# Attention and a routed layer of eight experts on one core: narrower buffer waits, a late search of four bits a step, splits and fillers placed anew

## The chip, the core and the metric

The kernel runs on one core of a Trainium2 chip. A time is that of one execution on the device in microseconds (us). Before the change three runs gave 829.34, 824.45 and 827.95 us, a median of 827.95. One more execution was taken with the profiler.

## What is computed

The reference first computes causal attention with a position bias for 8 batches of 8 heads, 576 positions and 64 columns. The result is viewed as 4608 tokens of 512 columns, and a routed layer follows:

```python
logits = x @ w_gate                      # 4608 tokens, 8 experts
order = np.argsort(-logits.flatten())    # best pair of token and expert first
for idx in order:                        # each expert takes at most 576 tokens
    tok, e = idx // E, idx % E
    if assigned[tok] >= 0 or counts[e] >= cap: continue
    assigned[tok] = e; counts[e] += 1
for e in range(E):
    mask = assigned == e
    out[mask] = np.maximum(x[mask] @ w1[e], 0) @ w2[e]   # 512 -> 1024 -> 512
```

The assignment is sequential in the reference. The kernel finds it one expert at a time: which expert fills first, and at which logit.

## The kernel before, in words

**Order of the work.** The program is written out by a planner (`Plan`). Each instruction or small group is a task with an engine, a duration, dependencies, buffers from a `Ring`, a priority (the lower number goes first) and sometimes a slack or a hold. The planner simulates the engines. When an engine comes free it starts the task that can start soonest; the priority decides only between tasks that can start at the same moment, and after that the order in which they were entered. A task with a hold stands back if one of lower number will be ready within that time. The order so found is the order of each engine's queue on the chip, where instructions wait in turn.

**Attention** (`Attention`) runs to about 350 us. At its end `xout` stores the last batch's rows in HBM (`xs`, L616 and L618), `turn` forms the router's logits, and `batch_tasks` takes each token's best expert and the sort key's first digit (`choose`, L788 to L809). The router's constants are made by GpSimd early in attention (`consts`, L730), one after the other (`build`, L669).

**Routing** (`Router.phase`, L836) is done eight times, once per expert j, with one plan for routing and experts together. It searches the key at which an expert reaches its 576 tokens, seven steps of at most five bits (`BITS`). A step, on VectorE and TensorE in turn: compare the 40 token columns with 32 candidate digits (`ge`, L886, 1280 elements); ten matmuls count per candidate and expert (L909); copy the counts (`ca`, L913); four matmuls with `qb` add up four parts (L918); compare with the places left (`pe`, L921); one matmul counts candidates (L923); take the largest (`jc`, L926); subtract (`wd`, L930). Beside this chain `digits` cuts the next digits (L813) and L897 prepares `y`. Then the expert's number `ei` is known (L861). A prefix matmul (L982, L983) and `places` (L1018) turn marks into token numbers: VectorE steps, ten matmuls (L1051), a copy, four matmuls (L1058), and `ids` (L1065). A bookkeeping chain (L996 to L1014) and the next phase's `choose` run beside it. For j of 2 and more, search matmuls get a slack of 0.45 us (`SLACK`), so the planner sets them that much after their operands.

**Experts** (`Moe.expert`, L1090). SyncE reads `ei` and loads twelve pieces of that expert's weights (L1134). ScalarE makes the high halves (L1138), VectorE the low halves (L1141); both have priority 2 + j. GpSimd gathers the tokens by `ids` in five tiles, four of 128 and one of 64 (L1103). For expert 0 TensorE transposes each tile (L1118) and ScalarE copies it; for the others a transposing DMA on SyncE does (L1110). The first layer (`first`, L1159) has eight units of 12 matmuls of 512 columns (L1169), each followed by one of 64 for the fifth tile (L1173). With `split`, only for expert 0, three of the units are begun tile by tile as tiles arrive, in matmuls of 128 columns. Then `relu`, and the second layer (L1240, L1243), whose results GpSimd scatters (L1223).

**Filler.** `route_and_experts` (L1267) enters sixteen matmuls that compute nothing (L1280) after the first placement.

**Memory.** Attention's pools are closed before the router's and experts' pools (`Router.pools`, L724; `Moe.__init__`, L1078) are opened over the same bytes. A pool opened in the plain way makes its first users wait until all tiles of the pools that it lies over are done with.

Of the kernel before, what the change touches and what calls it, by code (L numbers as in the profile page):

```python
# [9 lines left out]
F32 = mybir.dt.float32  # L10
F16 = mybir.dt.float16
# [193 lines left out]
class Attention:  # L205
# [454 lines left out]
    def build(self):  # L660
# [8 lines left out]
        for dur, f in self.router.consts():  # L669
            x = pl.add("p", dur, f, [x], prio=3)  # L670
# [26 lines left out]
J = 32  # L697
BITS = (5, 5, 5, 5, 5, 5, 2)
# [3 lines left out]
SLACK = (0.0, 0.15, 0.45)  # L702
NONE = 1.0e9
NT = 8 * S


class Router:
# [3 lines left out]
    def __init__(self, tc, ctx, L):  # L711
        self.tc, self.nc, self.L = tc, tc.nc, L
        c = self.c = ctx.enter_context(tc.tile_pool(name="rc", bufs=1))
# [7 lines left out]
        self.dg = c.tile([128, len(BITS), NC_], I32, name="dg")  # L721
        self.w0 = c.tile([128, NC_], BF, name="w0")

    def pools(self, ctx):  # L724
        P = lambda name, bufs, **k: ctx.enter_context(self.tc.tile_pool(name=name, bufs=bufs, **k))
        self.w = P("rw", 1)
        self.out = P("ro", 1)
        self.ps = P("rps", 1, space=PSUM)

    def consts(self):  # L730
# [6 lines left out]
        def do(dur, f):  # L737
            todo.append((dur, f))
# [6 lines left out]
        self.kj = iota([128, J, 4], [[1, J], [0, 4]], base=1, dt=BF, name="kj")  # L745
        self.Ws = iota([128, len(BITS), E], [[16, len(BITS)], [-1, E]], base=16 + E, name="Ws")
# [7 lines left out]
        self.quart = T([128, 128], F16, "quart")  # L754
        fill(self.quart, 16.0)
# [5 lines left out]
        for cc in range(4):  # L761
            do(0.35, lambda cc=cc: g.affine_select(
                self.qb[:, cc].rearrange("p (a b) -> p a b", a=4), on.rearrange("p (a b) -> p a b", a=4),
                pattern=[[0, 4], [-4, J]], base=-cc, channel_multiplier=1, compare_op=OP.is_equal, fill=0.0))
# [4 lines left out]
        do(0.35, lambda: g.tensor_copy(self.ident16, self.identf))  # L769
        fill(self.U, 1.0)  # L770
# [17 lines left out]
    def choose(self, c=slice(0, NC_)):  # L788
# [5 lines left out]
        B = [128, c.stop - c.start, E]  # L794
# [12 lines left out]
            (0.175, lambda: v.tensor_scalar(dg[:, 0], sg, 32 - BITS[0], None, op0=OP.logical_shift_right)),  # L807
# [3 lines left out]
    def digits(self, c):  # L811

        return [lambda s=s, n=n: self.nc.vector.tensor_scalar(  # L813
            self.dg[:, s, c], self.sg[:, c], 32 - sum(BITS[:s + 1]), 2 ** n - 1,
            op0=OP.logical_shift_right, op1=OP.bitwise_and) for s, n in enumerate(BITS) if s]

    def rings(self):
# [3 lines left out]
            ge=R(w, [128, NC_ // 4, J, 4], F16, "ge", 2), y=R(w, [128, NC_], F32, "y", 2),  # L821
            ca=R(w, [128, 4, E], F16, "ca", 2), pe=R(w, [128, E], F16, "pe", 2), wd=R(w, [128, NC_], BF, "wd", 2),
# [513 lines left out]
```

## Time and profile before

| what | value |
|---|---|
| median of three runs | 827.95 us |
| the profiled execution | 835.8 us, its span 834.1 us |
| busy share of the span | TensorE 89%, VectorE 73%, ScalarE 46%, GpSimd 42% |
| mean granted TensorE clock | 0.942 |

A stretch is read with its granted clock: TensorE has two levels, 1.2 and 2.4 GHz, shown as 0.5 and 1. A busy share is an average over a stretch, and what limits a stretch is seen from which wait ends last in it. In a row of the order of time the first number is the start in microseconds from the span's beginning, the second the duration of one instruction or of a merged run (x tells how many); brackets tell for how long the engine stood idle before it and what it waited for. `DVE` is VectorE, `PE` TensorE, `ACT` ScalarE, `POOL` GpSimd, `SP` SyncE.

### The profile page before, as it was taken

The page shows a single profiled execution, that of the slowest core. Times are in us where ns is not written, and L with a number is a line of the kernel's source. Part 1 is how long each engine was busy: PE and PEld are TensorE (multiplying, and loading weights), DVE is VectorE, ACT ScalarE, POOL GpSimd, SP SyncE. Part 2 cuts the span into 40 slices and gives each one's busy share as a digit, 9 for nine tenths or more (in the row PEclk, how much of TensorE's full clock was granted, in tenths as well). Part 3 has the DMA queues.
Part 4 walks back from the last instruction along what each step waited for, and adds up shares of the span by engine and source line. Part 5 has one row for each costly group of instructions (what it writes and reads, how often), then busy time and mean ns, then how long its engine had stood idle before and what let it go on. Part 6 is the DMA issues. An engine that isn't in the chain of part 4 may idle for free.

```text
span 834.1 us, 23171 instructions
## 1 busy us (share of the span) xinstructions
PE 740.5 (89%) x9059; PEld 466.9 (56%) x9059; DVE 605.6 (73%) x1992; ACT 379.8 (46%) x724; POOL 348.1 (42%) x423
## 2 busy tenths in 40 slices
PE   5288999999989999624999999999999799999995
PEld 1167777877778778512854545545555355454542
DVE  7679999999999997457885786867869568550110
ACT  2366877887768766503441233422334223441210
POOL 5178878878878888302013031121322112401011
PEclk8599999999999999855799999999999999999998
DMA  4955758685657511105238266392735937961001
GB/s 138 288 146 161 229 154 229 191 227 152 195 163 214 145 32 60 58 1 181 80 128 213 72 174 162 127 226 91 187 118 149 193 93 180 262 186 39 20 14 45
DMA packets 85316, 119.30 MB, mean 143 GB/s; under 512 B 40726, under 2 KB 57238, under 8 KB 85206
## 3 DMA queue, kind: packets, MB, share of 16 engines
q1 hardware_dynamic: 79318, 98.93, 43.3%
q0 software_dynamic: 5888, 18.88, 7.9%
q8 instruction: 71, 1.16, 0.6%
q14 instruction: 39, 0.32, 0.1%
HBM read 71.67 MB, written 19.10 MB: 109 GB/s over the span
## 4 chain that ended last, share of the span: by engine, by line
PE 44%; issue 18%; DVE 17%; DMA 5%; POOL 4%; ACT 1%; another core or an unknown queue 0%; SPq 0%; POOLq 0%; DVEq 0%; ACTq 0%
PE psm L1169 13%; PE psm L1243 10%; DVE scr L442 6%; DVE QK L381 3%; PE pst L514 2%; DMA xg<-xs,ids 2%; PE pst L515 2%; PE pss L473 2%; PE psm L1240 2%; PE psn L1173 2%; PE psa L909 2%; PE po L587 2%; POOL out_dram L1223 2%; PE po L589 2%; PE po L588 1%
## 5 line engine op out<-in xcount | busy, mean ns | idle before, releaser
L527 POOL TENSOR_TENSOR R<-P 128x512 f16<-128x512 f32 (+1 forms) x224 | 236.9, 1083 | 45.0 <-ACT P L525 43.9
L1169 PE MATMUL psm<-xT,w1p 128*128 128x512 f16 (+1 forms) x876 | 197.4, 358 | 0.0
L1243 PE MATMUL psm<-w2p,hT 128*128 128x512 f16 x768 | 178.5, 383 | 0.0
L1173 PE MATMUL psn<-xT,w1p 128*128 128x64 f16 x768 | 142.2, 193 | 0.0
L525 ACT ACTIVATE P<-pst 128x512 f32<-128x512 f32 (+1 forms) x224 | 117.6, 548 | 51.4 <-PE pst L517 26.7
L442 DVE CUSTOM_DVE_ANT_0 scr<-pss,mS 128x512 bf16<-128x512 f32 (+3 forms) x256 | 124.1, 485 | 12.2 <-PE pss L473 1.8
L1169 PEld LDWEIGHTS <-w1p 128*128 128x128 f16 x876 | 81.8, 100 | 80.1
L1103 POOL DMA_INDIRECT xg<-xs,ids x40 | 42.2, 1055 | 199.1 <-DVE sg L805 96.3
L1223 POOL DMA_INDIRECT out_dram<-y,ids x40 | 41.6, 1040 | 196.1 <-ACT y L1254 164.4
L1243 PEld LDWEIGHTS <-hT 128*128 128x128 f16 x768 | 70.3, 98 | 81.1 <-issue 5.4
L587 PE MATMUL po<-V,P 128*128 128x65 f16 x960 | 110.1, 195 | 2.3 <-DVE xp L608 1.8
L514 PE MATMUL pst<-QK 70*128 70x64 f16 (+4 forms) x512 | 105.4, 249 | 7.1 <-DMA QK<-mt 6.7
L589 PE MATMUL po<-V,R 128*128 128x65 f16 x960 | 110.2, 193 | 0.1
L588 PE MATMUL po<-Vl,P 128*128 128x64 f16 x960 | 109.9, 192 | 0.0
L515 PE MATMUL pst<-QK 128*128 128x64 f16 (+4 forms) x512 | 104.9, 248 | 0.0
L587 PEld LDWEIGHTS <-P 128*128 128x128 bf16 x960 | 89.6, 97 | 9.3 <-issue 6.7
L588 PEld LDWEIGHTS <-P 128*128 128x128 bf16 x960 | 89.1, 99 | 7.3 <-issue 3.5
L1189 ACT ACTIVATE hT<-psm 128x512 f16<-128x512 f32 x64 | 38.2, 597 | 119.1 <-PE psm L1169 94.8
L473 PE MATMUL pss<-QK 67*128 67x512 f16 (+3 forms) x256 | 72.9, 307 | 20.3 <-DVE mr L442 13.5
L589 PEld LDWEIGHTS <-R 128*128 128x128 f16 x960 | 89.1, 97 | 0.3 <-POOL R L527 0.3
L1173 PEld LDWEIGHTS <-w1p 128*128 128x128 f16 x768 | 72.8, 98 | 0.7
L1254 ACT ACTIVATE y<-psm 128x512 f32<-128x512 f32 x32 | 19.1, 596 | 114.5 <-PE psm L1243 103.6
(202 smaller groups left out, 1396.0 us busy)
## 6 DMA issues: line engine op xcount, KB each, us to landing
QK<-QK SPq DMA_DIRECT2D x120, 144.0 KB
wst<-in_w_dram SPq DMA_DIRECT2D x32, 512.0 KB
wst<-in_w_dram SPq DMA_DIRECT2D x64, 256.0 KB
rv<-in_v_dram SPq DMA_DIRECT2D x16, 576.0 KB
raw<-in_q_dram SPq DMA_DIRECT2D x15, 576.0 KB
raw<-in_k_dram SPq DMA_DIRECT2D x15, 576.0 KB
xs<-xp SPq DMA_DIRECT2D x8, 1024.0 KB
xs<-xp SPq DMA_DIRECT2D x8, 128.0 KB
```

Of the source, the lines that this page charges most:

```text
L442: return pl.add("v", dur, lambda: nc.vector.tensor_tensor_reduce(scr.t[:, :n], ps(), mask, 1.0, init() if init else -3e38, OP.add, OP.max, ...
L473: nc.tensor.matmul(ps.t[:, :n], F()[:, q0:q0 + 128], F()[:, k0:k0 + n], start=True, stop=True)
L514: nc.tensor.matmul(ps[:, c0:c0 + n], F()[:, ks:ks + 128], F()[:, q:q + n], start=True, stop=False)
L515: nc.tensor.matmul(ps[:, c0:c0 + n], G()[:, ks:ks + 128], G()[:, q:q + n], start=False, stop=not diag)
L525: e = pl.add("a", n / 1200 + 0.171, lambda: nc.scalar.activation(P.t[:, c0:c0 + n], ps.t[:, :n], AF.Exp, scale=1.0 / YS), [x] + fresh, pri ...
L527: sub = lambda eng: eng.tensor_tensor(R.t[:, c0:c0 + n], P.t[:, c0:c0 + n], strided_hi(P.t)[:, c0:c0 + n], op=OP.subtract)
L587: nc.tensor.matmul(o[:, i], H[:, c:c + 128], V.t[:, pr, sl], start=f, stop=False)
L588: nc.tensor.matmul(o[:, i, 0:64], H[:, c:c + 128], Vl.t[:, pr, sl], start=False, stop=False)
L589: nc.tensor.matmul(o[:, i], R.t[:, c:c + 128], V.t[:, pr, sl], start=False, stop=l)
L1169: nc.tensor.matmul(ps[:, tiles[0]:tiles[-1] + 1] if len(tiles) > 1 else ps[:, tiles[0]], lhs(f, c, a), xT.t[:, tiles[0]:tiles[-1] + 1, 4 * ...
L1173: nc.tensor.matmul(pt.t[:, 64 * f:64 * f + 64], lhs(f, c, a), xT.t[:, 4, 4 * b + c, 0:64], start=s, stop=e)
L1243: nc.tensor.matmul(py.t, hT.t[:, f, a, 128 * i:128 * i + 128], w2p.t[:, f, b], start=f == 0 and k == 0, stop=f == 7 and k == 2)
```

## The change

- Both pools over attention's memory are opened so that each tile waits only for those earlier tiles whose bytes it covers (`reuse_waits="tile"`).
- Search has two forms. Experts 0 and 1 keep 32 candidates, four columns at a time, seven steps. Experts 2 to 6 get 16 candidates, eight columns at a time, eight steps of four bits: `ge` of 640 elements, five count matmuls of 64 columns, a product with a constant mask (`own`) in place of the copy, one matmul with a constant (`same`) in place of four, a reduction (`sm`), then as before.
- The slack of search matmuls from the third phase on goes from 0.45 to 0.3 us.
- `places` of the first phase gets priority -1 instead of 0. The splits of expert 0's W1 get 0.5 instead of 2.
- `split` holds for experts 0 and 1.
- Filler: five matmuls after the first phase's last search matmul, fourteen after its prefix, twenty-eight after its placement, instead of sixteen after the placement.
- Three new constants are made on VectorE during attention, two more on GpSimd.

The diff, cut to its core:

```diff
-BITS = (5, 5, 5, 5, 5, 5, 2)
+FEW, MANY = (32, 4, (5, 5, 5, 5, 5, 5, 2)), (16, 8, (4,) * 8)
-SLACK = (0.0, 0.15, 0.45)
+SLACK = (0.0, 0.15, 0.3)
+PW_ = (0.5,)
...
     def pools(self, ctx):
-        P = lambda name, bufs, **k: ctx.enter_context(self.tc.tile_pool(name=name, bufs=bufs, **k))
+        P = lambda name, bufs, **k: ctx.enter_context(self.tc.tile_pool(name=name, bufs=bufs, reuse_waits="tile", **k))
...
+        J, G = self.forms[1].J, self.forms[1].G
+        self.own, self.same1, self.same = T([128, G], F32, "own"), T([128, J], F32, "same1"), T([128, 128], F16, "same")
+        v, one = nc.vector, self.identf.rearrange("p (j c) -> p j c", c=G)
+        do(0.29, lambda: v.tensor_reduce(self.own, one.rearrange("p j c -> p c j"), AX.X, OP.add), "v")
+        do(0.29, lambda: v.tensor_reduce(self.same1, one, AX.X, OP.add), "v")
+        do(0.29, lambda: v.tensor_copy(self.same.rearrange("p (a j) -> p a j", j=J),
+                                       self.same1[:, None, :].to_broadcast([128, 128 // J, J])), "v")
...
-            for s, n in enumerate(BITS):
+            for s, n in enumerate(form.bits):
...
+                def f_pa(gt=gt, A=A, n=n):
+                    for q in range(NC_ // G):
+                        nc.tensor.matmul(A.t[:G * n, 0:G * E], gt()[:, q].rearrange("p j c -> p (j c)"),
+                                         oh[:, G * q:G * q + G].rearrange("p c e -> p (c e)"),
+                                         start=(q == 0), stop=(q == NC_ // G - 1))
...
+                else:
+                    V(0.23, lambda ca=ca, counts=counts: v.tensor_tensor(
+                        ca.t, counts(), self.own[:, :, None].to_broadcast([128, G, E]), op=OP.mult), takes=[ca], uses=[A])
+                    pb = lambda s=s: B.t[:, 256 + G * E * (s % 2):256 + G * E * (s % 2 + 1)]
+                    T(0.035, lambda ca=ca, pb=pb: nc.tensor.matmul(
+                        pb(), self.same, ca.t.rearrange("p c e -> p (c e)"), start=True, stop=True),
+                      takes=[B] if s == 0 else (), uses=[ca] + ([B] if s else []))
+                    V(0.22, lambda sm=sm, pb=pb: v.tensor_reduce(sm.t, pb().rearrange("p (c e) -> p e c", c=G), AX.X, OP.add),
+                      takes=[sm], uses=[B])
+                    V(0.16, lambda pe=pe, sm=sm: v.tensor_tensor(pe.t, sm.t, self.rem, op=OP.is_ge), takes=[pe], uses=[sm])
...
-        self.places(pl, info, X, Y, placed, 0 if j < 2 else prio)
+        self.places(pl, info, X, Y, placed, -1 if j == 0 else 0 if j < 2 else prio)
...
-        P = lambda name, bufs, **k: ctx.enter_context(tc.tile_pool(name=name, bufs=bufs, **k))
+        P = lambda name, bufs, **k: ctx.enter_context(tc.tile_pool(name=name, bufs=bufs, reuse_waits="tile", **k))
...
+            pw = PW_[j] if j < len(PW_) and k < 4 else prio
...
-        split = ident is not None
+        split = j < 2
...
-    hot = Buf(R.r["C"])
-    warm = lambda: tc.nc.tensor.matmul(hot.t, R.ones, R.qb.rearrange("p c n -> p (c n)"), start=True, stop=True)
-    x = first["pi"]
-    for n in range(16):
-        x = pl.add("t", 0.43, warm, [x], prio=1.5, uses=[hot])
+    for tag, n, dur, ring in (("pc", 5, 0.43, M.r["ps"]), ("po", 14, 0.43, M.r["ps"]), ("pi", 28, 0.22, R.r["C"])):
+        x, hot = first[tag], Buf(ring)
+        for _ in range(n):
+            x = pl.add("t", dur, lambda hot=hot: tc.nc.tensor.matmul(
+                hot.t, R.ones, R.qb.rearrange("p c n -> p (c n)"), start=True, stop=True), [x], prio=1.5, uses=[hot])
```

## Rows read from the trace of the kernel before

**Rows 1.** The page's head: the profiled execution.
```profile
span 834.1 us, 23171 instructions
```

**Rows 2.** Busy time by stretch: PE, PEld, DVE, ACT, POOL, then granted clock, DMA, GB/s.
```profile
350.00:360.00 10.00, 1.70 (x34) 1.25 (x35) 4.96 (x27) 0.72 (x2) 0.00 (x0) 0.50 0.34 120
...
390.00:400.00 10.00, 6.57 (x59) 4.55 (x58) 5.14 (x15) 3.38 (x4) 4.43 (x4) 0.64 0.63 197
400.00:410.00 10.00, 9.72 (x152) 9.31 (x150) 8.30 (x22) 4.76 (x8) 0.00 (x0) 0.68 0.34 107
...
550.00:600.00 50.00, 49.49 (x420) 25.57 (x419) 39.41 (x132) 16.82 (x27) 11.04 (x14) 1.00 0.61 163
```

**Rows 3.** VectorE in order of time (start, duration), attention's end and first search.
```profile
353.05 0.16 DVE L809 CAST w<-dg 128x5 bf16<-128x5 int32 x1
356.17 0.82 DVE L886 TENSOR_TENSOR ge<-w,kj 128x1280 f16<-128x1280 bf16 x1 [2.96 <-DMA xs<-xp]
```

**Rows 4.** VectorE in order of time, second search beside expert 0's W1 splits.
```profile
389.54 0.68 DVE L1141 SCALAR_TENSOR_TENSOR w1p<-wst,w1p 128x512 f16<-128x512 f32 x1
...
396.06 0.19 DVE L913 CAST ca<-psa 128x32 f16<-128x32 f32 x1 [3.24 <-PE psa L909]
...
401.92 0.68 DVE L1141 SCALAR_TENSOR_TENSOR w1p<-wst,w1p 128x512 f16<-128x512 f32 x1
```

**Rows 5.** TensorE in order of time, expert 0's start (several queries).
```profile
397.24 1.03 PE L1118 MATMUL psm<-id,xg 128*128 128x128 f16 x8 [0.79 <-DMA xg<-xs,ids]
...
399.52 1.33 PE L1169 MATMUL psm<-xT,w1p 128*128 128x128 f16 x11
...
402.76 3.57 PE L1169 MATMUL psm<-xT,w1p 128*128 128x128 f16 x32
...
407.85 2.00 PE L1169 MATMUL psm<-xT,w1p 128*128 128x128 f16 x33
...
413.34 0.38 PE L1169 MATMUL psm<-xT,w1p 128*128 128x512 f16 x1
```

**Rows 6.** GpSimd in order of time, expert 0's gathers.
```profile
388.17 1.57 POOL L1103 DMA_INDIRECT xg<-xs,ids  x1 [44.24 <-DVE w L809]
...
394.49 0.91 POOL L1103 DMA_INDIRECT xg<-xs,ids  x1 [0.30 <-issue]
```

**Rows 7.** TensorE in order of time: placement at either clock; chain: late matmuls.
```profile
382.90 1.38 PE L1051 MATMUL psc<-rv,ol 128*128 128x144 bf16 x10 [2.75 <-DVE ol L1044]
...
634.97 0.79 PE L1051 MATMUL psc<-rv,ol 128*128 128x144 bf16 x10
...
494.53 2.39 PE psm L1243 x11
...
502.73 0.24 PE psa L909 x10
```

**Rows 8.** TensorE in order of time, later searches between expert matmuls.
```profile
543.90 0.24 PE L918 MATMUL psb<-ca,qb 128*128 128x8 f16 x4
544.01 1.02 PE L1243 MATMUL psm<-w2p,hT 128*128 128x512 f16 x4
...
639.34 0.19 PE L1173 MATMUL psn<-xT,w1p 128*128 128x64 f16 x1
639.37 0.38 PE L1169 MATMUL psm<-xT,w1p 128*128 128x512 f16 x1
```

**Rows 9.** TensorE's waits after 400 us: total, times, longest.
```profile
PE psa L909 <- DVE ge L886: 4.8, 1, 4.8
PE psb L918 <- DVE ca L913: 2.9, 3, 1.9
PE psb L923 <- DVE pe L921: 2.0, 2, 1.5
```

**Rows 10.** SyncE's last tile for expert 1, and TensorE's start of expert 1.
```profile
447.13 1.21 SPq L1110 DMA_TRANSPOSE xT<-xg  x1
...
460.10 0.22 PE psm L1169
```

More of the change, by code (lines that the diff above doesn't have):

```diff
@@ L753, in consts @@
         fill(on, 1.0)
-        self.quart = T([128, 128], F16, "quart")
-        fill(self.quart, 16.0)
+        for n, f in enumerate(self.forms):
+            f.share = T([128, 128], F16, f"share{n}")
+            fill(f.share, 64.0 * f.J / 128)
         self.tri = T([128, 128], F16, "tri")
@@ L793, in choose @@
         sg, dg, U, w0 = self.sg[:, c], self.dg[:, :, c], self.U[:, c], self.w0[:, c]
-        B = [128, c.stop - c.start, E]
+        B, bits = [128, c.stop - c.start, E], self.forms[form].bits
         W = self.W[:, None, :].to_broadcast(B)
@@ L916, in f_pb @@
-                def f_pb(ca=ca, n=n, s=s):
-                    for q in range(4):
-                        nc.tensor.matmul(B.t[:, 16 * s:16 * s + 8], self.qb[:4 * n, q], ca.t[:4 * n, q], start=(q == 0),
-                                         stop=(q == 3))
-                T(0.11, f_pb, takes=[B] if s == 0 else (), uses=[ca] + ([B] if s else []))
-                V(0.165, lambda pe=pe, s=s: v.tensor_tensor(pe.t, B.t[:, 16 * s:16 * s + 8], self.rem, op=OP.is_ge),
-                  takes=[pe], uses=[B])
@@ L923, in phase @@
-                T(0.03, lambda pe=pe, s=s: nc.tensor.matmul(pc(s), self.quart, pe.t, start=True, stop=True),
+                def f_pa(gt=gt, A=A, n=n):
[3 more added lines that the diff above has]
+                                         start=(q == 0), stop=(q == NC_ // G - 1))
+                T(0.16 if G == 8 else 0.28, f_pa, takes=[A], uses=[ge])
@@ new lines, in phase, with f_pb @@
+                counts = lambda A=A, n=n: A.t[:G * n, 0:G * E].rearrange("p (c e) -> p c e", c=G)
+                if G == 4:
+                    V(0.19, lambda ca=ca, counts=counts, n=n: v.tensor_copy(ca.t[:4 * n, 0:4], counts()), takes=[ca], uses=[A])
+                    def f_pb(ca=ca, n=n, s=s):
+                        for q in range(4):
+                            nc.tensor.matmul(B.t[:, 16 * s:16 * s + 8], self.qb[:4 * n, q], ca.t[:4 * n, q], start=(q == 0),
+                                             stop=(q == 3))
+                    T(0.11, f_pb, takes=[B] if s == 0 else (), uses=[ca] + ([B] if s else []))
+                    V(0.165, lambda pe=pe, s=s: v.tensor_tensor(pe.t, B.t[:, 16 * s:16 * s + 8], self.rem, op=OP.is_ge),
+                      takes=[pe], uses=[B])
+                else:
[8 more added lines that the diff above has]
+                    V(0.16, lambda pe=pe, sm=sm: v.tensor_tensor(pe.t, sm.t, self.rem, op=OP.is_ge), takes=[pe], uses=[sm])
@@ L924, in phase @@
+                info["pc"] = T(0.03, lambda pe=pe, s=s: nc.tensor.matmul(pc(s), form.share, pe.t, start=True, stop=True),
                   uses=[pe, B])
@@ L1142, in weights @@
                 dst.t[:, key, 1, c:c + 512], st.t[:, c:c + 512], sc, dst.t[:, key, 0, c:c + 512], op0=OP.mult,
-                op1=OP.subtract), [hi], prio=prio, uses=[st, dst], hold=0.35) for c in range(0, n, 512)]
+                op1=OP.subtract), [hi], prio=pw, uses=[st, dst], hold=0.35) for c in range(0, n, 512)]
             out[key] = (hi, lo)
```

72 lines of the change are left out of this document (35 added, 37 removed).

## The prediction, made before the changed kernel was seen

> **What bounds the kernel now.** I read the page's head first: the profiled execution spans 834.1 us [rows 1] and took 835.8 us in all; the three timed runs have a median of 827.95 us. The sum below is made against 835.8 and then scaled by 827.95/835.8 = 0.9906, because the durations come from that execution. Next I read busy time by stretch [rows 2]. The reader is to see two kinds of stretch. From about 410 us to the end TensorE is full (49.49 of 50 us in the stretch shown) at the full granted clock, 2.4 GHz; VectorE has slack there (39.41 of 50). In that stage only fewer TensorE cycles, or fewer of its waits, shorten the kernel. From 350 to 410 us it is the other way round: TensorE does 1.70 us of work in ten at the lower clock (0.50 granted, 1.2 GHz), then 6.57 and 9.72 with 0.64 and 0.68 granted. This is the passage from attention to the first expert, a chain of short steps over VectorE, TensorE, GpSimd and DMA; whatever is cut from it comes off the end, because the full stage behind it starts earlier.
>
> The order of time then shows three things in the passage. First, the search's opening comparison waits 2.96 us for the landing of attention's last rows in HBM, though the digit it needs was made at 353.05 + 0.16 = 353.21 [rows 3]. Second, in the second search VectorE stands for 3.24 us behind TensorE, which stands in order behind token tiles that are still arriving; so the last split of expert 0's W1 starts at 401.92 while the first started at 389.54 [rows 4]. Third, expert 0's first layer begins at 399.52, and its first step of full width, for which all five tiles are needed, at 413.34 [rows 5].
>
> **The change part by part.**
>
> *Buffers wait for their own bytes.* The comparison tile lies over attention's constants, not over the rows being stored, so with the narrower wait it should follow the digit at once: 356.17 - 353.21 less a hop, 2.9 us [rows 3]. Ends: 0, if another byte under it is late too, and 2.96. A loss is excluded, for no wait is added. I take 2.9, since the row names the store as the only thing waited for. Everything behind it moves along: first ids, weight loads (they hang on the expert's number) and gathers. Next late is the search itself, unchanged for expert 0 and 1 (seven steps of five bits).
>
> *First ids ahead.* The placement of expert 0 gets a lower priority number, but it alternates on VectorE with the bookkeeping chain because each link leaves a hop, and the planner fills the hop with whatever is ready. I cost it at nothing (cover: that alternation); if the planner did set it ahead, it would be worth part of the rival with the better start.
>
> *Warm-up and W1 splits ahead.* Before, sixteen filler matmuls came after the placement; now five follow the search, fourteen the prefix and twenty-eight the placement. They sit in TensorE's idle time (1.70 of 10 us busy [rows 2]). Placement at the higher clock takes 0.79 us where it now takes 1.38: 0.6 us [rows 7]. The eight half-splits of W1 get priority 0.5, equal to the digits of the second search, and were entered before those, so they win the tie. They take 8 x 0.68 = 5.4 us, and from 389.54 would be through at 395.0 rather than at 402.6 [rows 4]. Then TensorE's own order is late: the third tile's transposes are planned ahead of the first expert matmul and stand at 397.24 + 1.03 = 398.3 [rows 5]. From there to full width it has 4 tiles x 3 units x 12 = 144 matmuls of 128 columns, 36 of 64 columns and about three search steps. At the higher clock 33 of the first kind take 2.00 us, 0.06 each; at the lower 32 take 3.57, 0.11 each [rows 5]. So 144 x 0.06 + 36 x 0.03 + 3 x 0.38 = 10.9, and full width comes at 409.2, 4.1 us earlier than 413.34. Ends: if all of it ran at the lower clock, 144 x 0.11 + 2.2 = 18.0 and 416.3, 3 us later; if tile order did not hold it, 395.0 + 10.9 = 405.9, 7.4 us earlier. I take 4.1: part of the stretch already runs high (0.68 [rows 2]) with far less filler, which is nearer to the higher end. With placement 4.7 us.
>
> The splits now stand on VectorE beside GpSimd's gathers. The gather issued while VectorE was busy took 1.57 us, the last, with VectorE idle, 0.91 [rows 6]; five of them at the longer price would be 3.3 us. The Trainium skill (SBUF — State Buffer, "SBUF: two separate sides") says VectorE and GpSimd share a port pair by an exclusive lock, and that GpSimd cannot write gather descriptors while VectorE holds it. By that rule the order chosen here would slow the gathers, and the gain of 4.7 would shrink to 1.4; the two rows agree in direction, though the splits are not the only work beside them. I keep 4.7, as the third tile, not the last, sets the start.
>
> *Late search of four bits a step* (experts 2 to 6, five searches). Now a step is ten count matmuls, 0.24 us [rows 7], four that gather the counts, 544.01 - 543.90 = 0.11, and one, which I price like a 64-column matmul, 639.37 - 639.34 = 0.03 [rows 8]: 0.38, and seven steps 2.66 us. The new step has five matmuls of 64 columns, one more of 64 with the constant product mask, and one small: 7 x 0.03 = 0.21, and eight steps 1.68. Saved 0.98 x 5 = 4.9 us, in a stage where TensorE is full, so it comes off the end. Ends: 1.3, if five wide ones take as long as ten narrow (0.24 + 0.06 = 0.30 a step), and 6.6, if each costs the 0.024 of a narrow one. I take 0.03, a row of the same width.
> On VectorE the comparison halves (0.82 us [rows 3] to about 0.45) and a reduction (the planner books 0.22 us) and an eighth step come in. A search grows by one to two microseconds, covered by VectorE's 10 idle us in 50 [rows 2]. If that cover went, one late search would hold an expert.
>
> *Slack 0.45 to 0.3.* Search matmuls stand 0.15 us nearer to their operands in TensorE's order. Before, only six waits of 9.7 us in all are charged to such visits after 400 us [rows 9], long ones that 0.15 would not decide. Nothing, with the rival below as the other end.
>
> *Expert 1 by tiles.* Three units of 12 matmuls of 512 columns become four times as many of 128: 144 x 0.06 = 8.6 [rows 5] instead of 36 x 2.39/11 = 7.8 [rows 7]: +0.8 us (0 to 1). It guards against tiles arriving late; today the last tile is issued by 448.3 and expert 1 starts at 460.10 [rows 10]. If expert 0 ends 2.9 + 4.7 = 7.6 us earlier, at 452.5, that tile, 2.9 earlier at least, is still in time.
>
> *Constants.* One more iota and fill on GpSimd and three short VectorE operations, once, early in attention: nothing, at most 1 us (five of about 0.2, as the short rows in [rows 3, 4]); the loads of the first heads cover them.
>
> **Sum:** 2.9 + 4.7 + 4.9 - 0.8 = 11.7 us; 835.8 - 11.7 = 824.1, and by 0.9906 816 us, 1.4% faster. The waits of [rows 9] I leave as they are: they are tied to moments, and every moment moves.
>
> **The rivals.**
>
> *A. The early gain is caught.* Expert 0 runs ahead, but expert 1's ids, which hang on a VectorE that is nearly full there (8.30 of 10 us [rows 2]), do not; TensorE waits. For it: 3.24 us of VectorE standing in that search [rows 4] and splits now ahead of its digits. Against: some 7 us of room [rows 10]. Without the 4.7: 828.8, 821 us. Chance 0.17.
>
> *B. A better start and no long waits.* Tiles do not hold the splits (7.4 + 0.6) and the 9.7 us of waits [rows 9] go: 2.9 + 8.0 + 4.9 - 0.8 + 9.7 = 24.7, 811.1, 803 us. Chance 0.12.
>
> *C. Slower: the searches stop TensorE.* Eight steps with three visits each in five searches are 120 visits. TensorE works in order, so each late visit stops it. If each is late by just the 0.15 us of slack removed, 18 us are lost: 842.1, 834 us. It decides from 11.7/120 = 0.10 us a visit. Against: VectorE has room and most visits now cost nothing [rows 9]. Chance 0.08.
>
> *D. Gathers held by VectorE.* All five at 1.57 us [rows 6] push the tiles back by 3.3: gain 8.4, 827.4, 820 us. Chance 0.10. This is what the Trainium skill's rule above would make of it.
>
> *E. The change does not do what it says early on.* Something else under the pools is as late as the store, and the splits cannot come ahead for want of loaded weights: only 4.9 - 0.8 = 4.1 is left, 831.7, 824 us. Chance 0.10.
>
> **How the numbers follow.** My forecast has the remaining 0.43, with 813 to 821 from the ends of its terms, one at a time, the wholly low clock left out. About 0.5%, or 4 us (824 to 832), is what a measurement of this kernel can tell from no change. Faster by more: nearly all of the forecast, A, B and D, and half of E, 0.81; within: half of E and edges, 0.11; slower: C, 0.08. The range 804 to 827 takes in A, D, E and the nearer half of B, and leaves out C.
>
> **What would show it.** In the changed profile the first comparison should follow the digit without a store in between; the granted clock should be above 0.64 in the ten microseconds before the first expert matmul; the last W1 split should come before the third tile's transposes; full width about 7.6 us after the move, near 406; a late step should have five counts and take about 0.21 of TensorE. It is wrong if full width does not come earlier by more than 3 us, if TensorE gets many short waits on search lines (C), or if a new wait stands before expert 1 (A).

## The result and the profile after

The changed kernel took 817.02 us, the median of four runs (816.37 to 817.13), beside 827.37 us for the kernel before (four runs, 824.45 to 829.34): ratio 0.9876, 95% interval 0.9845 to 0.9907. The forecast was 816. The profiled execution took 816.4 us. It lies at the median, whereas the profile before lay 8 us above its own.

Busy time by stretch, the columns and three of the stretches of [rows 2]:

```profile
390.00:400.00 10.00, 8.64 (x168) 8.31 (x168) 7.26 (x25) 7.48 (x12) 0.00 (x0) 1.00 0.56 171
400.00:410.00 10.00, 10.00 (x161) 6.97 (x159) 8.57 (x23) 2.91 (x6) 0.00 (x0) 1.00 0.01 4
550.00:600.00 50.00, 48.95 (x375) 24.70 (x374) 42.44 (x150) 16.39 (x27) 10.76 (x15) 1.00 0.58 162
```

The first expert now starts at the full granted clock, 1.00 (2.4 GHz) where it was 0.64 and 0.68. In the full stage VectorE has 42.4 busy us of 50, 3.0 more than before.

VectorE in order of time, the places of [rows 3, 4]:

```profile
350.16 0.16 DVE L830 CAST w<-dg 128x5 bf16<-128x5 int32 x1
350.36 0.83 DVE L909 TENSOR_TENSOR ge<-w,kj 128x1280 f16<-128x1280 bf16 x1
...
385.67 0.19 DVE L938 CAST ca<-psa 128x32 f16<-128x32 f32 x1 [1.63 <-PE psa L932]
...
387.19 3.13 DVE L1177 SCALAR_TENSOR_TENSOR w1p<-wst,w1p 128x512 f16<-128x512 f32 x5
```

The comparison follows the digit with no store in between. The stand in the second search is 1.63 us instead of 3.24, and the last W1 split ends at 390.3, no longer 402.6.

TensorE in order of time, the first expert's start (against [rows 5]) and one late search step (against [rows 7, 8]):

```profile
390.15 0.38 PE L1205 MATMUL psm<-xT,w1p 128*128 128x128 f16 x4 [0.20 <-issue]
390.37 0.61 PE L1152 MATMUL psm<-id,xg 128*128 128x128 f16 x8
...
393.59 0.62 PE L1152 MATMUL psm<-id,xg 128*128 128x128 f16 x8 [1.21 <-DMA xg<-xs,ids]
...
402.96 0.38 PE L1205 MATMUL psm<-xT,w1p 128*128 128x512 f16 x1
...
483.13 0.31 PE L932 MATMUL psa<-oh,ge 128*128 128x64 f16 x5
483.27 1.03 PE L1279 MATMUL psm<-w2p,hT 128*128 128x512 f16 x4
485.56 0.19 PE L951 MATMUL psb<-ca,same 128*128 128x64 f16 x1 [1.25 <-DVE ca L948]
485.59 1.24 PE L1279 MATMUL psm<-w2p,hT 128*128 128x512 f16 x5
```

Full width comes at 402.96 instead of 413.34. The starts of neighbours price the late step: 483.27 - 483.13 = 0.14 for five count matmuls, 0.03 for the matmul with the constant, and 0.03 for the last (487.93 - 487.90): 0.20.

TensorE's waits from 385 us on (total, times, longest), against [rows 9]:

```profile
PE psb L951 <- DVE ca L948: 3.7, 3, 1.4
PE psb L957 <- DVE pe L956: 2.0, 3, 1.1
PE psa L932 <- DVE ge L909: 1.7, 1, 1.7
PE psb L957 <- issue: 1.6, 1, 1.6
...
PE psa L1016 <- POOL X L1007: 0.7, 1, 0.7
```

After 400 us, behind the first expert's tiles, these are 9.7 us again, the sum of [rows 9], but in other places. What they are, the experiments had to tell.

### The profile page after: what moved, and what is told of

The parts are those of the page before. It is cut to its first block, busy times and chain, and to the rows that moved or that the text cites. A ratio compares the mean times of both kernels' runs of the same rounds, so it can differ in the third digit from the quotient of the medians.

```text
span 814.7 us, 23030 instructions
## 1 busy us (share of the span) xinstructions
PE 734.8 (90%) x8953; PEld 466.2 (57%) x8953; DVE 608.4 (75%) x2070; ACT 379.3 (47%) x724; POOL 344.5 (42%) x425
## 4 chain that ended last, share of the span: by engine, by line
PE 60%; issue 17%; DVE 13%; DMA 4%; POOL 3%; ACT 1%; SPq 1%; another core or an unknown queue 0%; POOLq 0%; DVEq 0%; ACTq 0%
PE psm L1205 14%; PE psm L1279 13%; DVE scr L442 5%; PE pst L514 4%; PE pst L515 4%; PE pss L473 3%; PE po L587 3%; PE po L589 3%; PE po L588 3%; PE psm L1276 2%; PE psn L1209 2%; POOL out_dram L1259 2%; PE pss L635 2%; PE pss L457 1%; POOL xg L1137 1%
## 5 line engine op out<-in xcount | busy, mean ns | idle before, releaser
L527 POOL TENSOR_TENSOR R<-P 128x512 f16<-128x512 f32 (+1 forms) x224 | 232.7, 1065 | 52.5 <-ACT P L525 51.6
L1205 PE MATMUL psm<-xT,w1p 128*128 128x512 f16 (+1 forms) x984 | 193.8, 333 | 0.2 <-issue 0.2
L1279 PE MATMUL psm<-w2p,hT 128*128 128x512 f16 x768 | 174.8, 379 | 0.0
L525 ACT ACTIVATE P<-pst 128x512 f32<-128x512 f32 (+1 forms) x224 | 118.9, 548 | 51.8 <-PE pst L517 24.0
L1209 PE MATMUL psn<-xT,w1p 128*128 128x64 f16 x768 | 136.8, 193 | 0.0
L1137 POOL DMA_INDIRECT xg<-xs,ids x40 | 42.2, 1055 | 175.8 <-DVE val L827 68.0
L587 PE MATMUL po<-V,P 128*128 128x65 f16 x960 | 114.1, 196 | 2.5 <-DVE xp L608 2.0
L514 PE MATMUL pst<-QK 70*128 70x64 f16 (+4 forms) x512 | 109.6, 253 | 7.1 <-DMA QK<-mt 7.1
L589 PE MATMUL po<-V,R 128*128 128x65 f16 x960 | 114.2, 194 | 0.0
L588 PE MATMUL po<-Vl,P 128*128 128x64 f16 x960 | 113.8, 193 | 0.0
L515 PE MATMUL pst<-QK 128*128 128x64 f16 (+4 forms) x512 | 108.1, 252 | 0.0
L588 PEld LDWEIGHTS <-P 128*128 128x128 bf16 x960 | 90.2, 100 | 8.1 <-issue 3.2
L587 PEld LDWEIGHTS <-P 128*128 128x128 bf16 x960 | 90.6, 98 | 6.2 <-issue 2.7
L473 PE MATMUL pss<-QK 67*128 67x512 f16 (+3 forms) x256 | 73.8, 311 | 17.8 <-DVE mr L442 10.1
```

Source lines behind the costliest of these rows:

```text
L473: nc.tensor.matmul(ps.t[:, :n], F()[:, q0:q0 + 128], F()[:, k0:k0 + n], start=True, stop=True)
L514: nc.tensor.matmul(ps[:, c0:c0 + n], F()[:, ks:ks + 128], F()[:, q:q + n], start=True, stop=False)
L515: nc.tensor.matmul(ps[:, c0:c0 + n], G()[:, ks:ks + 128], G()[:, q:q + n], start=False, stop=not diag)
L525: e = pl.add("a", n / 1200 + 0.171, lambda: nc.scalar.activation(P.t[:, c0:c0 + n], ps.t[:, :n], AF.Exp, scale=1.0 / YS), [x] + fresh, pri ...
L527: sub = lambda eng: eng.tensor_tensor(R.t[:, c0:c0 + n], P.t[:, c0:c0 + n], strided_hi(P.t)[:, c0:c0 + n], op=OP.subtract)
L587: nc.tensor.matmul(o[:, i], H[:, c:c + 128], V.t[:, pr, sl], start=f, stop=False)
```

## The experiments

The twelve runs were made in three lots, each on one chip with its own runs of the kernel before. This table gives the milestones, each from the order of time of the run's profile. **Attention** is from the first score matmul (L514) to the last gate matmul (L645); **search** is the first comparison; **full** the first matmul of 512 columns of expert 0; **last** the last matmul of an expert. The bracketed numbers are distances to the milestone before.

| run | attention | search | full | last | median us | ratio to before (95%) |
|---|---|---|---|---|---|---|
| before, first profile | 39.8 to 351.1 | 356.2 | 413.3 (57.2) | 824.2 (410.9) | 827.37 | |
| after, first profile | 41.8 to 348.2 | 350.4 | 403.0 (52.6) | 804.6 (401.7) | 817.02 | 0.9876 (0.9845 to 0.9907) |
| e0_again | 38.8 to 351.9 | 356.9 | 414.1 (57.1) | 811.4 (397.3) | 822.95, one | lot 1: before 822.73 |
| e1_pool | 42.0 to 349.0 | 352.1 | 403.9 (51.8) | 796.1 (392.3) | 808.16 | 0.9825 (0.9766 to 0.9884) |
| e2_few | 41.3 to 346.0 | 348.1 | 399.8 (51.7) | 798.5 (398.7) | 813.24 | 0.9892 (0.9834 to 0.9950) |
| e3_petr | 42.1 to 346.6 | 348.7 | 400.6 (51.9) | 820.4 (419.8) | 832.26 | 1.0125 (1.0063 to 1.0187) |
| e9_after | 42.2 to 351.8 | 353.9 | 405.8 (51.8) | 797.6 (391.8) | 807.56 | 0.9810 (0.9774 to 0.9847), lot 2: 822.31 |
| e4_fill | 45.5 to 356.1 | 358.3 | 413.6 (55.4) | 807.0 (393.4) | 809.69 | 0.9835 (0.9795 to 0.9876) |
| e5_nopw | 40.8 to 347.8 | 349.9 | 404.6 (54.7) | 795.1 (390.5) | 807.15 | 0.9812 (0.9772 to 0.9852) |
| e8_bpool | 40.8 to 355.0 | 357.1 | 414.2 (57.1) | 810.8 (396.6) | 820.48 | 0.9970 (0.9941 to 0.9999) |
| e10_after | 41.8 to 348.4 | 350.6 | 402.1 (51.5) | 793.7 (391.6) | 805.41 | 0.9770 (0.9730 to 0.9810), lot 3: 824.19 |
| e11_consts | 41.7 to 348.9 | 351.9 | 408.3 (56.4) | 807.2 (398.9) | 817.89 | 0.9926 (0.9897 to 0.9955) |
| e6_slack | 41.7 to 348.8 | 350.9 | 403.0 (52.1) | 806.9 (404.0) | 819.39 | 0.9946 (0.9917 to 0.9975) |
| e7_split0 | 41.4 to 345.2 | 347.4 | 399.6 (52.2) | 793.0 (393.4) | 806.99 | 0.9792 (0.9755 to 0.9830) |

### Both kernels again: whose waits are they?

**e0_again** is the kernel before, unchanged; **e9_after** and **e10_after** are the changed kernel.

> The kernel before once more, unchanged, with a second profile. Theory: the profiled execution of before, 835.8 us, held a chance wait of 5 us before 662 us that its timed runs (824 to 829) mostly do not have; a second profile then spans about 827 us, the wait at TensorE's count matmuls (4.8 us) is gone or short, and attention's last digit stands at 353 us again. Rival: the wait belongs to the program; then the span is again 833 to 835 us with a wait of about 5 us at the same place.

> The changed kernel once more, beside the kernel before on the same chip, as the base for the next three runs. Theory (waits of one to two microseconds behind TensorE results come and go from chip to chip and run to run, the plan does not decide them): the ratio stays near 0.988, but the waits after full width are not the 10.7 us of its first profile; they lie between 0 and 5 us, and the time from full width to the last expert matmul is 391 to 397 us. Rival (the waits belong to the changed plan, because buffers that wait for their own bytes let transfers start in worse moments): 10 to 11 us of waits again, 401 to 402 us from full width to the last expert matmul, where the same kernel with pools that wait whole had 392.3.

> The changed kernel again, as the base for the next three on this chip. Theory (the waits of its first profile belong to that chip or that run, not to the plan): ratio 0.980 to 0.988; from first comparison to full width 51.8 to 52.6 us. Rival (they belong to the plan): more than 8 us of waits after full width.

TensorE's waits from 385 us on, in e0_again:

```profile
PE psm L1118 <- DMA xg<-xs,ids: 3.8, 3, 1.8
PE psc L1058 <- ACT pc L1054: 0.5, 1, 0.5
PE psb L923 <- DVE pe L921: 0.4, 1, 0.4
PE psc L1280 <- DVE pf L1062: 0.3, 1, 0.3
PE psb L918 <- DVE ca L913: 0.3, 1, 0.3
```

And in e10_after:

```profile
PE psm L1152 <- DMA xg<-xs,ids: 0.9, 1, 0.9
PE psa L1016 <- POOL X L1007: 0.7, 1, 0.7
PE psb L957 <- DVE pe L956: 0.2, 1, 0.2
```

The first line of each is the first expert waiting for its tiles, before full width. The 4.8 us wait of [rows 9] is gone from the same program, and so are the long ones of the changed kernel: after 400 us, behind those tiles, 0.7 us is left in e0_again, 0.9 in e10_after and 1.2 in e9_after. So neither plan makes the long waits by itself. The theories of the three runs came in the waits; the times came out lower than they had, with a span of 821.2 us for about 827 and ratios of 0.9810 and 0.9770 for 0.988 and 0.980 to 0.988. The changed kernel took 807.6 and 805.4 us on these occasions instead of 817.0; the kernel before was 3 to 5 us lower there too. Whether the waits go with the chip or with the single execution is open: e9_after and e10_after ran on two chips, and the four executions of the first occasion lie within 0.8 us of each other. With the waits small in both, e0_again and e10_after differ by 6.3 us up to the search, 5.6 from there to full width and 5.7 from there to the last matmul, 17.6 in all.

One long wait can be followed to where it began, the 4.8 us of [rows 9] before 662 us. SyncE and ScalarE in order of time, in the kernel before and then in e0_again:

```profile
642.63 13.84 SPq L1110 DMA_TRANSPOSE xT<-xg  x4
...
659.47 0.63 ACT L1138 ACTIVATE w2p<-wst 128x512 f16<-128x512 f32 x1 [7.98 <-DMA wst<-in_w_dram]
```

```profile
636.13 8.48 SPq L1110 DMA_TRANSPOSE xT<-xg  x4
...
647.54 0.63 ACT L1138 ACTIVATE w2p<-wst 128x512 f16<-128x512 f32 x1 [2.64 <-DMA wst<-in_w_dram]
```

SyncE issues transposing DMAs and weight loads in one order, and each transposing DMA waits for its gather to land: 7.6 us in two waits here, 3.1 in e0_again. So the next weight load was issued 5.3 us later, ScalarE's half of it waited 5.3 us longer, VectorE's half stood behind that, and behind it the search that TensorE was waiting for. Why the gathers landed late is not known.

What makes the other waits long stays open. In the changed kernel's first profile they lie where SyncE has its transposing DMAs under way. At the first of them VectorE and ScalarE, which wait for different results of TensorE, go on together:

```profile
438.38 0.22 DVE L954 TENSOR_REDUCE sm<-psb 128x8 f32<-128x64 f32 x1 [2.17 <-PE psm L1276]
438.41 0.60 ACT L1290 ACTIVATE y<-psm 128x512 f32<-128x512 f32 x1 [6.89 <-PE psm L1276]
```

In e10_after VectorE does not wait there and ScalarE waits 4.96 us. So the delay is not VectorE's own, though TensorE then waits for VectorE; what held both is not known. One run tried the transposing DMAs. **e3_petr** transposes on TensorE for all experts:

```diff
-        behind = M.expert(pl, j, info, behind, R.ident16 if j == 0 else None)
+        behind = M.expert(pl, j, info, behind, R.ident16)
```

> The changed kernel, but the tokens of experts 1 to 7 are transposed by TensorE and copied by ScalarE, as those of expert 0 are, and SyncE issues no transposing DMA. Theory: the waits of 1 to 2 us that TensorE shows once or twice per expert all lie in stretches where transposing DMAs are being issued and are tied to them; without them most of the 11 us go, against 7 times 40 small matmuls of about 0.056 us (15.7 us more TensorE work): about 822 us, with hardly a wait over 0.45 us after expert 0. Rival: the waits come from the gathers or from VectorE's order; then they stay at 8 to 11 us, and the kernel takes about 832 us.

It took 832.26 us, with waits of another kind:

```profile
PE psm L1152 <- DMA xg<-xs,ids: 8.0, 14, 1.9
```

TensorE now stands for the gathers themselves, 14 times, and does the transposes besides (busy 749.5 us against 733.0 in e10_after). The theory's 822 did not come. The rival's 832 did, but out of other parts: beside e1_pool on the same chip, which has no long waits and took 808.16 us, TensorE is busy for 17.8 us more (731.7 there), and the waits for gathers are 8.0. The waits on the search's lines are absent, but e9_after and e10_after lost them with the transposing DMAs in place. So these DMAs alone do not make them; whether they take part is not shown either way.

### The pools

**e8_bpool** is the kernel before with the pools' change alone; **e1_pool** is the changed kernel without it:

```diff
-        P = lambda name, bufs, **k: ctx.enter_context(self.tc.tile_pool(name=name, bufs=bufs, **k))
+        P = lambda name, bufs, **k: ctx.enter_context(self.tc.tile_pool(name=name, bufs=bufs, reuse_waits="tile", **k))
```

> The kernel before with one part of the change alone: buffers in both pools wait for their own bytes. Theory (as predicted): the first comparison follows the digit at once, 0.1 us behind it instead of 2.9 to 3.0, all milestones behind it move 2.9 us forward, and the time is 2 to 4 us below the kernel before, ratio about 0.9965. Rival 1 (the move is caught by the next late thing, ids or gathers or tiles): the wait is gone, but full width comes less than 1 us earlier and the time is the same. Rival 2 (the wider freedom costs something in the full stage, waits of one to two microseconds): full width earlier, but full width to the last expert matmul longer than the 397 to 398 us of the undisturbed kernel before, time the same or above.

> The changed kernel, but both pools wait whole again. Theory (the sum's first term): the first comparison waits again about 3 us for the store of the last rows, everything behind moves along, and the kernel takes 2.9 us more, about 820 us. Rival: the passage has room elsewhere (gathers, weight loads), and less than 1 us comes back, 817 to 818 us.

VectorE in order of time, in e8_bpool and then in e1_pool:

```profile
356.91 0.16 DVE L809 CAST w<-dg 128x5 bf16<-128x5 int32 x1
357.11 0.83 DVE L886 TENSOR_TENSOR ge<-w,kj 128x1280 f16<-128x1280 bf16 x1
```

```profile
352.08 0.82 DVE L909 TENSOR_TENSOR ge<-w,kj 128x1280 f16<-128x1280 bf16 x1 [1.02 <-DMA xs<-xp]
```

In the order of before the wait of 2.97 us (e0_again) goes. The ratio of 0.9970 is 2.5 us (0.1 to 4.9), which holds the predicted 2.9 but does not tell it from much less; attention began 1.9 us later in this profile and took 1.2 us longer, so the milestone itself did not move. In the new order of attention the store that the plain pools wait for has almost landed: there the wait is 1.0 us (0.96 in e11_consts), and that is what the part is worth by the profile. Its worth in time is not shown, for the changed kernel itself did not run on e1_pool's chip. The 808.16 us of e1_pool lie below both sides on record, which were reckoned from the 817 of the first occasion.

### The constants

**e11_consts** is the kernel before plus the new constants, which nothing new uses:

```diff
+        j_, G = 16, 8
+        self.own, self.same1, self.same = T([128, G], F32, "own"), T([128, j_], F32, "same1"), T([128, 128], F16, "same")
+        do(0.29, lambda: v.tensor_reduce(self.own, one.rearrange("p j c -> p c j"), AX.X, OP.add), "v")
...
```

> The kernel before with the new constants alone, made in the same order as in the changed kernel and used by nothing new. Over the profiles so far attention takes 311.3 to 314.2 us from its first score matmul to its last gate matmul in the kernels with the old constants and 304.5 to 310.6 in those with the new, while its start comes 1 to 4 us later. Theory: the constants alone do this, because the planner, which books them on GpSimd and VectorE beside attention's first heads, then picks another order for all of attention: this run has 304 to 310 us there, starts later by 1 to 2 us, and is 2 to 5 us faster than the kernel before, ratio 0.994 to 0.998; everything behind attention stays (57 us from first comparison to full width, 396 to 398 from there to the last expert matmul). Rival (as predicted, the constants cost nothing to 1 us and attention's difference is chance): 311 to 314 us, ratio 1.000 to 1.001.

TensorE in order of time, attention's first score matmul and its last gate matmuls, in e0_again and then in e11_consts:

```profile
38.84 0.58 PE L514 MATMUL pst<-QK 70*128 70x512 f16 x1 [5.33 <-DMA QK<-mt]
...
351.55 0.48 PE L645 MATMUL po<-wgp,xt 128*128 128x8 f16 x13 [0.39 <-ACT xt L638]
```

```profile
41.72 0.59 PE L514 MATMUL pst<-QK 70*128 70x512 f16 x1 [7.28 <-DMA QK<-mt]
...
348.52 0.51 PE L645 MATMUL po<-wgp,xt 128*128 128x8 f16 x13 [0.38 <-ACT xt L638]
```

Attention takes 307.1 us instead of 313.0 (311.3 and 314.2 in the two other profiles with the old constants, 303.8 to 310.6 in all eleven with the new), and the run is faster by 0.74%, 6.1 us (3.7 to 8.5), a little more than the theory's 2 to 5. TensorE's order throughout attention is that of the changed kernel, instruction for instruction (5590 matmuls), and differs from that of the kernel before from the 40th on: five short constants, booked in the planner's queues beside the first heads, made it pick another order for almost the whole of attention, and in that order attention is shorter. Up to the search e11_consts is 5.0 us ahead of e0_again: 5.9 from the shorter attention and 2.0 from a shorter wait for the store (0.96 us instead of 2.97), less 2.9 of a later start. The bracket in the first row of each is the wait for the first score's operands, brought by DMA. It is 5.33 and 7.28 us here, 7.26 in e8_bpool with the old constants and 11.18 in e4_fill with the new, so some microseconds of a single profile's milestones are chance, and the distances between them are the safer reading. The table shows the start of attention at 38.8 to 40.8 us with the old constants and at 40.8 to 45.5 with the new, so some 2 us of the shorter attention are given back ahead of it.

### The first expert's start

**e4_fill** has the old filler, **e5_nopw** the splits of W1 at their old priority:

```diff
-    for tag, n, dur, ring in (("pc", 5, 0.43, M.r["ps"]), ("po", 14, 0.43, M.r["ps"]), ("pi", 28, 0.22, R.r["C"])):
+    for tag, n, dur, ring in (("pi", 16, 0.43, R.r["C"]),):
```

```diff
-PW_ = (0.5,)
+PW_ = ()
```

> The changed kernel with the filler of before (sixteen matmuls, after the placement only), the W1 splits still ahead. The disputed term is the 4.6 us between the first comparison and full width (57.2 before, 52.6 after). Theory: most of it hangs on the clock, since TensorE, not VectorE, is what the first expert waits for once the splits are ahead; at the lower clock the placement takes 0.6 us longer and the 144 short matmuls of the first expert part of their way 0.11 instead of 0.06 us: first comparison to full width 54.5 to 57, total 2 to 4 us above the changed kernel on this chip. Rival: the transposes and first matmuls raise the clock soon enough by themselves: first comparison to full width 52.6 to 53.3, total within 1 us.

> The changed kernel without the priority of the first expert's W1 splits (they stand behind the second search's steps again), the new filler kept. Theory: the last split ends some 8 to 12 us later than 390.3, about 10 to 12 us before full width as in the kernel before (402.6 against 413.3), so first comparison to full width is 54.5 to 57 us and the total 2 to 4 us above the changed kernel. Rival: with TensorE at the higher clock VectorE no longer stands 3.2 us in the second search, the splits fill its gaps anyway and are through by 394; then the tiles set the start and nothing is lost: 52.6 to 53.3, total within 1 us.

From search to full width they take 55.4 and 54.7 us against 51.8 in e9_after: 3.6 and 2.9 lost, where the three profiles of the changed kernel itself spread from 51.5 to 52.6. With the old filler the granted clock from 390 to 400 us is 0.67 and the first expert matmul waits until 400.95, though the splits are through at 395.7: it stands behind the third tile's transposes, which start at 399.70 after a wait for their gather. From there to full width it takes 12.7 us, within the 11.4 to 12.8 of those three, so the loss does not lie in the short matmuls, where the theory had most of it. The profile of e4_fill is also that of an execution of 818.84 us, 9 above the median of that run. With the old priority the clock is 1.00, the first matmul starts at 390.60 and the last split ends at 395.5, 45.6 us after the search: 4 to 6 later than in the changed kernel's profiles, where the theory had 8 to 12. So the passage lost what both theories said, but by neither path as they told it. In time e4_fill is 1.3 us above e9_after (808.88, without the profiled execution), e5_nopw 0.4 below (its rival had within 1); the intervals overlap, so what reaches the end of the kernel is not settled here, least of all for the splits.

### The late search and the slack

**e2_few** gives all searches the old form; **e6_slack** restores the old slack:

```diff
-            for dur, f in self.choose(form=int(j > 1)):
+            for dur, f in self.choose(form=0):
...
-            form = self.forms[j > 1]
+            form = self.forms[0]
```

```diff
-SLACK = (0.0, 0.15, 0.3)
+SLACK = (0.0, 0.15, 0.45)
```

> The changed kernel, but experts 2 to 6 search as experts 0 and 1 do: 32 candidates, seven steps. Theory (the sum's third term): 4.9 us of TensorE come back in the full stage, about 822 us. Rival: the longer VectorE chain of the new step brings waits of its own at TensorE that eat most of it; then the change back costs 0 to 2 us, 817 to 819 us, and the waits over 0.45 us before search matmuls, 11 us in the changed kernel's profile, fall.

> The changed kernel with the planner's slack for search matmuls back at 0.45 us. Theory (as predicted, 0.15 us decides nothing): the time within 1.5 us of the changed kernel, and the sum of TensorE's idle time charged to search lines behind full width within 1 us of it. Rival (each of 120 visits is late by up to 0.15 us at the smaller slack): the time 3 us or more below the changed kernel, with fewer short waits on the lines of the search.

The old form costs 738.0 us of TensorE where e1_pool has 731.7, and 813.24 us where it has 808.16: 6.3 us of busy time, 5.1 of time, close to the 4.9 predicted. But e1_pool lacks the pools' part too. Against e9_after and e10_after, on other chips, full width to the last matmul is 6.9 and 7.1 us longer in e2_few, with about 1 us of waits in each of the three. So the new form is worth 5 to 7 us. The times on record, 822 and 817 to 819, were reckoned from the 817 of the first occasion, and both missed.

The slack was the surprise: 819.39 us instead of 805.41, so 14 us for a number that I had priced at nothing. VectorE in order of time, the first comparisons of four late searches in a row and the eighth of the last, in e10_after and then in e6_slack:

```profile
429.52 0.49 DVE L909 TENSOR_TENSOR ge<-w,kj 128x640 f16<-128x640 bf16 x1
...
475.91 0.49 DVE L909 TENSOR_TENSOR ge<-w,kj 128x640 f16<-128x640 bf16 x1
...
524.52 0.49 DVE L909 TENSOR_TENSOR ge<-w,kj 128x640 f16<-128x640 bf16 x1
...
571.51 0.49 DVE L909 TENSOR_TENSOR ge<-w,kj 128x640 f16<-128x640 bf16 x1
...
598.45 0.49 DVE L909 TENSOR_TENSOR ge<-wd,kj 128x640 f16<-128x640 bf16 x1
```

```profile
430.42 0.49 DVE L909 TENSOR_TENSOR ge<-w,kj 128x640 f16<-128x640 bf16 x1
...
483.96 0.56 DVE L909 TENSOR_TENSOR ge<-w,kj 128x640 f16<-128x640 bf16 x1
...
536.80 0.49 DVE L909 TENSOR_TENSOR ge<-w,kj 128x640 f16<-128x640 bf16 x1
...
588.48 0.49 DVE L909 TENSOR_TENSOR ge<-w,kj 128x640 f16<-128x640 bf16 x1
...
620.04 0.49 DVE L909 TENSOR_TENSOR ge<-wd,kj 128x640 f16<-128x640 bf16 x1
```

From one search to the next it takes 46.4, 48.6 and 47.0 us with the slack of 0.3, and 53.5, 52.8 and 51.7 with 0.45. One expert takes TensorE 391.6/8 = 49.0 us in e10_after. So at 0.3 the routing chain just fits beside an expert; at 0.45 it is the longer of the two, and TensorE runs out of work before each new expert. Its waits in e6_slack:

```profile
PE psa L932 <- DVE ge L909: 4.5, 5, 1.1
PE psb L951 <- DVE ca L948: 1.7, 2, 1.3
PE psn L1209 <- DMA xT<-xg: 1.6, 1, 1.6
```

All its waits after 400 us add up to 10.4 us (0.9 in e10_after), of the 12.4 by which full width to the last matmul grew. Both sides on record missed: the theory had no difference, the rival a gain. The slack does not only keep TensorE from arriving early; it is added to the chain at every visit. From the first comparison to the eighth, seven steps, it takes 598.45 - 571.51 = 26.9 us with 0.3 and 620.04 - 588.48 = 31.6 with 0.45, 0.66 more a step; three visits at 0.15 us are 0.45 of it. What adds the other 0.2, in an order that was planned anew, is not shown, and only these two values of the slack were run.

The same view shows what the four-bit form costs: in e2_few, with the same slack, the late searches start 41.9 to 43.9 us apart. The new form saves TensorE 5 to 6 us and lengthens the chain by about 5 us a search, and only the smaller slack makes room for that.

### Expert 1 by tiles

**e7_split0** begins only the first expert by tiles:

```diff
-        split = j < 2
+        split = j < 1
```

> The changed kernel with only the first expert begun by tiles of tokens; the second runs its first layer whole. Theory (as predicted, narrow matmuls cost 0.8 us and guard against late tiles that are in time anyway): 0.8 us less from full width to the last expert matmul, no wait before the second expert's first matmul; time 0.8 us lower, which the timing can hardly tell. Rival (expert 0 now runs ahead of the second expert's last tile): a wait of 1 to 5 us on a transposing transfer before the second expert, time 1 to 4 us higher.

It took 806.99 us beside 805.41, intervals overlapping. The width of the matmuls can't be told in the time. Full width to the last matmul took 1.8 us more (393.4 for 391.6), where the theory had 0.8 less. Instead of the wait for a late tile that the rival named (0.2 us is left of it) the search stands in the way, with the longest wait behind full width:

```profile
PE psa L932 <- DVE ge L909: 0.9, 1, 0.9
```

None of the variants is faster than the changed kernel by more than its interval.

## Why the prediction was right, and where it was not

The total came out within its range, 817 against 816. By parts it was a sum of terms that mostly came, the gain of the constants left out, two steps on the search's chain that failed and cancelled, and chance waits that took back what the forecast lacked.

- **Buffers, 2.9.** The mechanism is right: the wait was 2.97 and goes. Its size holds only in the old order of attention; in the new order, which the change also brings, the wait is 1.0.
- **Constants, "nothing, at most 1 us".** This step failed. It priced the five operations by their durations and their cover, but they also enter a planner, and the plan of 310 us of attention changed: 6.1 us faster. That is the largest gain of the change not forecast; 2.0 us of it are wait for the store that the term above had counted.
- **First ids ahead, nothing.** From search to the last of the first ids it takes 381.7 - 350.4 = 31.3 us, 30.8 before. In line with it, though no run changed this priority alone.
- **Warm-up and splits, 4.7.** The size came, 57.2 - 52.6 = 4.6, and 5.3 and 5.6 in the later runs. The path was another: the third tile did not hold the start. The first expert matmul came at 390.15, 39.8 us after the search instead of the 42.1 worked out, and full width then took 12.8 us instead of 10.9, with the fourth tile late by 1.21 us. Each half of the edit, taken away, costs the passage 3.6 and 2.9 us in one profile each; together they bring less than the sum.
- **Gathers beside the splits, rival D.** GpSimd in order of time, the first and the last of the five gathers, to set beside [rows 6]:

```profile
382.73 1.75 POOL L1137 DMA_INDIRECT xg<-xs,ids  x1 [41.62 <-DVE w L830]
...
389.00 0.92 POOL L1137 DMA_INDIRECT xg<-xs,ids  x1 [0.30 <-issue]
```

  The five took 1.75 + 0.96 + 1.24 + 1.09 + 0.92 = 5.96 us, with five splits in a row on VectorE beside the last two. Before, they took 1.57 + 1.01 + 1.56 + 0.95 + 0.91 = 6.00, with VectorE busy for 5.14 of 10 us [rows 2]. The last of the five, wholly beside splits, took 0.92 us (0.91 and 1.07 in e10_after and e9_after), and before, with VectorE idle, 0.91. So the gathers did not take the 1.57 us each of rival D. The Trainium skill (SBUF — State Buffer, "SBUF: two separate sides") ties the lock on writing descriptors to VectorE's two-port modes, and sets an instruction with two inputs from SBUF, as these splits are, only against a GpSimd instruction that reads SBUF. The prediction had left out these conditions; no run here shows whether a gather falls under the second.
- **Late search, 4.9.** Right in its mechanism, and perhaps too small: 5 to 7 us, with a step of 0.20 us for the 0.21 worked out.
- **"A search grows by one to two microseconds, covered by VectorE's 10 idle us in 50", and the slack at nothing.** These two steps failed together and cancelled. The search grows by about 5 us at an equal slack. VectorE's idle share is no measure of the cover: what counts is the length of the chain against one expert, and in the kernel before they were already nearly equal (e0_again: 48.1 to 50.5 us from search to search, 397.3/8 = 49.7 an expert). The condition was named, "if that cover went, one late search would hold an expert"; e6_slack shows it coming true. I had looked for the slack in TensorE's waits [rows 9], where it can't appear: it sits in the chain as planned time.
- **Expert 1 by tiles, -0.8.** Neither shown nor refuted.
- **Waits of [rows 9] left as they are.** By luck: they were 9.7 us in both first profiles and a tenth of that in later ones. The profile before took 8 us more than its own median, and the profile after did not, so the timed runs of the changed kernel seem to have carried the waits and most of those before not; that took some microseconds off the gain. With the waits gone the forecast was too high: 0.9810 and 0.9770 were measured against the 0.986 predicted, and the constants are most of the difference.
- **Rivals.** A fell: in e10_after no wait stands before expert 1, and the lead at full width is kept to the end. B was half right: the tiles did not hold the start, and the long waits are absent in later runs; but the kernel before is lower there too, and 0.9810 and 0.9770 lie between the forecast and B's 803/827.95 = 0.970. D fell by the gathers. C fell: with the slack cut, 0.9 us of waits are left in e10_after. E fell by the first milestones.

## What to carry to other kernels

When a serial chain over two engines runs beside a full engine, compare the chain's period with the work it hides behind, and not the idle share of its engines. A slack put into a planned order is paid at every visit of the chain, and it shows as no wait until the chain becomes the longer one. In a kernel written out by a planner, an edit that costs nothing by its durations can still replan a distant stage; compare the order of instructions there before the gain is put down to the edit itself. And take a second profile of both kernels before a wait of microseconds is read as part of the plan.

## What was not expected of the hardware

The same program had 9.7, 1.2 and 0.9 us of TensorE waits after 400 us in three profiles, taken on three occasions, and medians of 817.0, 807.6 and 805.4 us; the kernel before had 9.7 and then 0.7. After the two longest waits of the kernel before TensorE ran at a lower granted clock for a while (0.66 from 446 to 451 us, 0.72 from 662 to 668), and its full stage took 13.6 us more than in e0_again for 9.0 us more of waits. The wait for attention's first operands was 5.3 to 7.6 us in thirteen profiles and 11.2 in one. Five gathers took the same time, 5.96 and 6.00 us, with more or fewer splits on VectorE beside them.
